# Key chunks that coincide with the query tiles, in an attention and feed-forward kernel on one core

## The chip, the cores and the metric

The kernel runs on one core of a Trainium2 chip. The core has a matrix engine (TensorE, "PE" in the profile, its loads of weights "PEld"), three engines for elementwise work (VectorE "DVE", ScalarE "ACT", GpSimd "POOL") and a queue that issues DMAs (SyncE, "SP"). TensorE writes only into eight PSUM banks of 128 partitions by 512 floats. The metric is the device time of one execution in microseconds; the program's own span, from its first to its last instruction, is what the trace covers.

## The reference

```python
scores = q @ k.T / sqrt(64)                    # 8 batches, 8 heads, 576 positions, 64 wide
decay  = cum[..., :, None] - cum[..., None, :] # cum = cumsum(log(clip(f)))
scores = where(causal, -1e9, scores + decay)
attn   = exp(scores - max); attn = attn / (sum(attn) + 1e-9)
x      = (attn @ v)                            # heads side by side: 4608 tokens, 512 wide
h      = x @ w_in                              # 512 to 2048
out    = softplus(h) @ w_out                   # 2048 to 512
```

All of it is float32. A product in which float32 precision is wanted is split: each operand is a rounded high part plus a low part, and three of the four part products are summed (a "fp32r" operand is a rounded part).

## The kernel before

The kernel is a list of operations, each with an engine (or a choice of engines), an estimated cost, its predecessors, and the buffers that it takes and gives back. A planner (`Plan.run`) walks this list with its estimated clocks and emits the operations in the order in which they would start; what it fixes is the order on each engine, and semaphores do the rest on the chip. So an operation's estimated cost (`on_turn`, `on_act`, `on_dve`, `on_pe`) changes the order, not the time that the chip takes.

The batches' heads come as jobs. Batch 0 is done in halves (`first`, `rest`, plain float32); batches 1 to 7 give 56 jobs `whole`, one head each. Between the steps of the jobs, units of the feed-forward part (`ffn_block`: ten blocks of 256 or 512 tokens, products of 512 columns into the banks `h` and `acc`) are let in by a budget. Their products stand between those of the heads in TensorE's queue.

A whole head runs thus. Five query tiles (`QT`, L249) of 64, 128, 128, 128, 128 rows are scored against all keys up to their own end (L756, L757, bank `s`), VectorE adds the mask and takes the row's extreme (L761), ScalarE takes the exponential into `p` (L781), and ScalarE, VectorE or GpSimd divides by the sum (L803, L805). Tile i ends at key 64, 192, 320, 448 or 576.

Then `weights(bi)` turns `p` round, one bank `b` at a time: `turn` (L849) transposes blocks on TensorE, with a block of `p` as the stationary operand and an identity (`ident`) as the moving one. `halves` is an identity whose halves are exchanged: a block turned against it lands 64 columns away, which is needed where a key chunk begins in the middle of a query tile. From the bank, `hi_part` (L861, copies at L211) makes the rounded high part `ph`, and `lo_part` the rest `pl` (L871) on VectorE. `output(gi)` (L891) multiplies the values `vhl` (high and low side by side, 128 columns, as the stationary operand) with `ph` and `pl` as the moving operands into a bank `o` (L911). Group 0 are queries 0 to 63, group 1 the rest. Two copies then put the result together in `x` (L934, L940).

Key chunks begin at 0, 128, 256, 384 and 512 and so lie across the query tiles. `banks` in `whole` (L541) lists, per bank, (first key, first query, last query, chunk of values):

- bank 0, the small one: keys 0 to 63 for queries 0 to 63, and keys 512 to 575 for queries 512 to 575, 64 columns each. Only 64 partitions are used, and the low part goes to partitions 64 to 127 of the same `ph64` tile (L868), so that one product takes both parts; for this the values' chunk `NCH` holds keys 0 to 63 twice (L615 to L618), and so does the last chunk of the padded `vR`.
- bank 1: keys 0 to 127, queries 64 to 575, 512 columns.
- bank 2: keys 128 to 255, queries 128 to 575, 448 columns.
- bank 3: keys 256 to 383 and 384 to 511, 320 and 192 columns.

Banks of PSUM named `att` (four) serve scores, transposes and outputs; `ph` and `pl` have three buffers each, `ph64` two. The values are loaded by three SyncE DMAs (L614, and two at L618) and split into high and low part (L687, L690). In the order of the list a head's first three banks are followed by group 0, the last bank and group 1, between the scores of the next head.

Of the kernel before, what the change touches and what calls it, by code (L numbers as in the profile page):

```python
# [10 lines left out]
F32 = mybir.dt.float32  # L11
U32 = mybir.dt.uint32
F32R = mybir.dt.float32r
# [34 lines left out]
class Plan:  # L48
# [161 lines left out]
def copy(e, out, in_):  # L210
    (e.tensor_copy if hasattr(e, "tensor_copy") else e.copy)(out, in_)  # L211
# [3 lines left out]
def tile_decay_attention_softplus_ffn(  # L215
# [18 lines left out]
    B, D, H, _, S = qkT.shape  # L234
    NT, DM = out.shape
    DFF = w_in.shape[1]
    P = 128
# [3 lines left out]
    NCH = vR.shape[3]  # L241
# [4 lines left out]
    LAG = 2  # L246
# [5 lines left out]
    BUFS = dict(T=2, att=4, h=2, acc=2, fe=4, ph=3, pl=3, ph64=2, gh=LAG + 1, gl=LAG + 1, xh=1, xl=1,  # L252
                x32=2, wl=2, vhl=3, vraw=1, raw=1)
    plan = Plan(BUFS | dict(T0=4, stat=4, p=2, xh0=1, xh1=1, xl0=1))
    add, give = plan.add, plan.give
# [7 lines left out]
    psum = ctx.enter_context(tc.tile_pool(name="psum", bufs=1, space=bass.MemoryType.PSUM))  # L263
# [15 lines left out]
    T = {}  # L279
# [15 lines left out]
    ps = [[cpool.tile([P, w], F32, name=f"p{i}_{w}") for w in PW] for i in range(2)]  # L295
# [242 lines left out]
    def whole(b, h):  # L538


        banks = [[(0, 0, 64, NCH), (512, 512, S, 4)], [(0, 64, S, 0)], [(128, 128, S, 1)],  # L541
                 [(256, 256, S, 2), (384, 384, S, 3)]]
        return dict(
            b=b, heads=[h], q=(0, S), k=(0, S), nv=NCH + 1,
            tiles=[(q0, n, 0, i, 0) for i, (q0, n) in enumerate(QT)],
            banks=banks, groups=[(0, 64, h, 0), (64, S, h, 64)],
        )
# [27 lines left out]
    def attention(job):  # L575
# [5 lines left out]
        plain = number < nplain  # L581
# [21 lines left out]

        def load_v():
            def v(e):
                shape = [P, (NCH + 1) * (2 if vtag == "vhl" else 1), D]
                vr = st["vr"] = buf(vtag, shape, f"vr{n}")[:, 0:nv]
                if pair:
                    e.dma_start(
                        out=vr[:, 0:4].rearrange("p (h c) d -> p h c d", h=2),  # L610
                        in_=vR[b, heads[0] : heads[0] + 2, :, 0:2].rearrange("h p c d -> p h c d"),
                    )
                else:
                    e.dma_start(out=vr[:, 0:NCH], in_=vR[b, heads[0]])  # L614
# [12 lines left out]

# [183 lines left out]


        parts = []
        used = {i: [] for i in range(len(banks))}
        tags = {}

        def weights(bi):
            spans, w = [], 0
            for key, lo, hi, vc in banks[bi]:
                spans.append((key, lo, hi, vc, w))  # L820
                w += hi - lo

# [26 lines left out]
            def turn(e):  # L849
                box["ps"] = bank("att", f"b{n}_{bi}")  # L850
                for x, at, one in blocks:
                    e.transpose(box["ps"][0 : x.shape[1], at : at + one.shape[1]], x, one)  # L852

            def keep(e):
                box["p"] = buf(tag, [P, 512], f"p{n}_{bi}", F32R)[:, 0:w].bitcast(F32)
                copy(e, box["p"], box["ps"][:, 0:w])

            more, size = ("64", P) if small else ("", 512)
            rows = 64 if small else P

            def hi_part(e):  # L861
                box["h"] = buf("ph" + more, [P, size], f"ph{n}_{bi}", F32R)[:, 0:w]
                copy(e, box["h"][0:rows], box["ps"][0:rows, 0:w])

            def lo_part(e):
                if small:
                    h = box["h"]
                    e.tensor_sub(h[64:P], box["ps"][0:64, 0:w], h[0:64].bitcast(F32))  # L868
                    return
                box["l"] = buf("pl", [P, size], f"pl{n}_{bi}", F32R)[:, 0:w]  # L870
                e.tensor_sub(box["l"], box["ps"][:, 0:w], box["h"].bitcast(F32))  # L871
# [6 lines left out]
            on = [on_act(w, psum=True), on_dve(w)]  # L878
# [12 lines left out]
        def output(gi):  # L891
            g0, g1, h, tok = groups[gi]
# [60 lines left out]
            if gi == len(groups) - 1:  # L953
                if plain:
                    give("T0", st["scores"])
                    if number == nplain - 1:
                        give("x32", cum_used)
                    give(st["vtag"], st["ends"])
                    for bi, ops in used.items():
                        give(tags[bi], ops)  # L960
                else:
                    give("T", st["scores"])
                    give("vhl", st["ends"])
                    for bi, ops in used.items():
                        if banks[bi][0][:3] == (0, 0, 64):
                            give("ph64", ops)
                        else:
                            give("ph", ops)
                            give("pl", ops)

        def loads():
# [492 lines left out]
```

## Time and profile before

| | |
|---|---|
| three executions | 1197.27, 1197.46, 1198.01 us (median 1197.46) |
| span of the profiled execution | 1196.2 us, granted TensorE clock 1.00 |
| TensorE matmuls | 6122 |
| chain that ended last | TensorE 77%, VectorE 12%, ScalarE 4%, DMA 3% of the span |
| DMA | 172.01 MB, mean 144 GB/s |

The span is the program's own; the time of an execution contains a little ahead of it and behind it, 1.3 us by the median. A row of the timeline has the start, the duration, the engine, the line, the operation, output<-inputs, the form, and the number of like instructions in a row. The duration of a pipelined matmul reaches past the start of the next one, so that TensorE's time is read from the distance of starts. In a row of groups stand, after the bar, the busy time in all, the mean of one in nanoseconds, and after the next bar the idle time of that engine just ahead of them with what ended it. In a row of stretches stand the bounds, the length, the busy time of each engine shown (with its number of instructions), the granted clock, the share of the DMA engines and GB/s.

### The profile page before, as it was taken

Reading aid. Unit: us, or ns where it says so; the run is one execution under the profiler, and the core shown is the slowest. Engines: PE = TensorE matmul, PEld = TensorE weight load, DVE = VectorE, ACT = ScalarE, POOL = GpSimd, SP = SyncE. Lnnn points to the kernel's source line nnn. Section 1 sums busy time; section 2 is a strip of 40 time slices with the busy share of each in tenths; the row PEclk is TensorE's granted clock in tenths of the full one; section 3 lists DMA queues with packets and bytes.
Section 4 is the critical chain, followed back from the end, with each engine's and each line's share of the span. In section 5 each row is a group of like instructions: output and inputs, shape, how many; then the busy total and the mean of one; then the engine's idle time right before and its main releaser. Section 6 shows DMA issues by size and latency. Waiting matters only on the chain.

```text
span 1196.2 us, 19275 instructions
## 1 busy us (share of the span) xinstructions
PE 1177.1 (98%) x6122; PEld 969.0 (81%) x6122; DVE 851.4 (71%) x2085; ACT 852.5 (71%) x2033; POOL 140.3 (12%) x143
## 2 busy tenths in 40 slices
PE   8999999999999999999999999999999999999998
PEld 6666678878888888888888888888888888888887
DVE  7998999897787778777787778677867773223322
ACT  6676888888886778678777778688867773444543
POOL 3200011111111110102011101011111110000000
PEclk9999999999999999999999999999999999999999
DMA  7855655545555645655565546555465524211210
GB/s 215 255 171 162 183 152 155 131 135 155 143 160 166 177 131 147 182 162 155 143 187 158 147 130 187 149 162 147 146 181 151 156 81 136 89 36 53 88 53 35
DMA packets 107317, 172.01 MB, mean 144 GB/s; under 512 B 20256, under 2 KB 77616, under 8 KB 107216
## 3 DMA queue, kind: packets, MB, share of 16 engines
q1 hardware_dynamic: 107200, 170.78, 50.1%
q8 instruction: 48, 0.79, 0.3%
q14 instruction: 53, 0.43, 0.1%
q10 hardware_dynamic: 16, 0.01, 0.0%
HBM read 126.49 MB, written 35.95 MB: 136 GB/s over the span
## 4 chain that ended last, share of the span: by engine, by line
PE 77%; DVE 12%; ACT 4%; DMA 3%; issue 2%; POOL 1%; SPq 0%; DVEq 0%; POOLq 0%; ACTq 0%
PE h L1069 27%; PE acc L1154 27%; PE b L852 7%; PE o L911 5%; PE s L756 3%; PE s L757 3%; DVE s L761 2%; PE h L1050 2%; PE acc L1173 1%; POOL p L805 1%; ACT p L781 1%; DMA raw<-in_qkT 1%; PE s L754 1%; PE o L905 1%; DVE T L712 1%
## 5 line engine op out<-in xcount | busy, mean ns | idle before, releaser
L1069 PE MATMUL h<-xh,wih 128*128 128x512 f32 (+1 forms) x576 | 229.1, 401 | 0.0
L781 ACT ACTIVATE p<-s,negm 128x288 f32<-128x288 f32 (+7 forms) x384 | 182.6, 478 | 55.0 <-DVE negm L761 53.4
L1069 PE MATMUL h<-xl,wih 128*128 128x512 f32 (+1 forms) x576 | 216.8, 379 | 0.0
L805 POOL TENSOR_SCALAR p<-p,rsum 64x64 f32<-64x64 f32 (+4 forms) x106 | 119.1, 1133 | 742.9 <-DVE rsum L794 292.5
L1116 DVE SCALAR_TENSOR_TENSOR h<-h,e 128x512 f32<-128x512 f32 x136 | 95.1, 699 | 138.1 <-ACT e L1108 137.3
L761 DVE CUSTOM_DVE_ANT_0 s<-s,cmask 128x288 f32<-128x288 f32 (+5 forms) x320 | 137.2, 439 | 74.1 <-PE s L757 63.6
L1102 ACT ACTIVATE e<-h 128x512 f32<-128x512 f32 x144 | 85.4, 594 | 112.7 <-PE h L1069 106.8
L1154 PE MATMUL acc<-woh_dt_float32r,gh 128*128 128x512 f32 x376 | 153.1, 407 | 0.1
L1069 PE MATMUL h<-xh,wl 128*128 128x512 f32 (+1 forms) x576 | 148.6, 380 | 0.0
L1154 PE MATMUL acc<-woh_dt_float32r,gl 128*128 128x512 f32 x376 | 147.3, 392 | 0.0
L1154 PE MATMUL acc<-wol_dt_float32r,gh 128*128 128x512 f32 x376 | 147.0, 391 | 0.0
L871 DVE TENSOR_TENSOR pl<-b,ph 128x512 fp32r<-128x512 f32 x168 | 110.8, 664 | 29.5 <-ACT ph L211 27.5
L211 ACT CAST ph<-b 128x512 fp32r<-128x512 f32 (+2 forms) x180 | 88.6, 500 | 50.8 <-PE b L852 47.4
L1069 PEld LDWEIGHTS h<-xh,wl 128*128 128x128 f32 x576 | 104.9, 188 | 21.5
L1069 PEld LDWEIGHTS h<-xh,wih 128*128 128x128 f32 x576 | 108.8, 189 | 15.5 <-PE b L852 0.2
L1069 PEld LDWEIGHTS h<-xl,wih 128*128 128x128 f32 x576 | 108.9, 189 | 14.7 <-DVE xl L1021 0.4
L852 PE MATMUL b<-ident,p 128*128 128x128 f32 (+1 forms) x728 | 117.8, 270 | 2.6 <-DVE x L940 0.6
L1124 DVE TENSOR_TENSOR gl<-h,gh 128x512 fp32r<-128x512 f32 x136 | 93.5, 687 | 36.6 <-ACT gh L211 36.0
L211 ACT CAST gh<-h 128x512 fp32r<-128x512 f32 x117 | 68.6, 586 | 53.6 <-DVE h L1116 48.1
L803 ACT ACTIVATE p<-p,rsum 128x320 f32<-128x320 f32 (+7 forms) x190 | 97.4, 573 | 5.1 <-DVE rsum L794 4.6
L756 PE MATMUL s<-T 128*64 128x64 f32 x336 | 98.5, 304 | 1.5 <-ACT p L781 1.3
L852 PEld LDWEIGHTS b<-ident,p 128*128 128x128 f32 (+1 forms) x728 | 86.1, 138 | 16.4 <-ACT p L781 2.1
(154 smaller groups left out, 2293.6 us busy)
## 6 DMA issues: line engine op xcount, KB each, us to landing
wl<-wil_d SPq DMA_DIRECT2D x72, 512.0 KB
raw<-in_qkT SPq DMA_DIRECT2D x112, 288.0 KB
g_d<-gh SPq DMA_DIRECT2D x84, 128.0 KB
g_d<-gl SPq DMA_DIRECT2D x84, 128.0 KB
vr<-in_vR SPq DMA_DIRECT2D x64, 160.0 KB
out<-ob SPq DMA_DIRECT2D x36, 256.0 KB
T<-T SPq DMA_DIRECT2D x56, 144.0 KB
sto<-in_w_out SPq DMA_DIRECT2D x11, 512.0 KB
```

Source lines behind the costliest of these rows:

```text
L211: (e.tensor_copy if hasattr(e, "tensor_copy") else e.copy)(out, in_)
L756: e.matmul(o, qA[:, q0:end], kA[:, a:z], start=True, stop=False)
L761: e.tensor_tensor_reduce(out=box["o"], in0=box["o"], in1=cmask[0:n_q, right - w : right], scale=-0.125, scalar=m0 if i else 3.0e38, op0=AL ...
L781: e.activation(o, box["o"], AF.Exp, bias=m1, scale=-1.0, accum_out=acc)
L803: e.activation(a, a, AF.Copy, scale=f_)
L805: e.tensor_scalar(a, a, f_, None, ALU.mult)
L852: e.transpose(box["ps"][0 : x.shape[1], at : at + one.shape[1]], x, one)
L871: e.tensor_sub(box["l"], box["ps"][:, 0:w], box["h"].bitcast(F32))
L1069: e.matmul(o, l, r, start=m == 0, stop=m == 11)
L1116: e.scalar_tensor_tensor(h, h, 0.0, box["e"], ALU.max, ALU.add)
L1124: e.tensor_sub(box["l"], box["t"], box["h"].bitcast(F32))
L1154: e.matmul(st["acc", tt], l, r[fc], start=first and m == 0, stop=last and m == 2,)
```

## The change

Key chunks of whole heads become 0 to 63, 64 to 191, 192 to 319, 320 to 447 and 448 to 575: the query tiles themselves. No block begins inside a query tile, and `halves` is left to the plain jobs. The first chunk has 64 keys and 512 later queries: its bank is `stacked` (high part in partitions 0 to 63, low part in 64 to 127, values doubled). Keys 0 to 63 for queries 0 to 63, the other part of that chunk, ride behind keys 320 to 447 in bank 1, with copies of their own (`first_hi`, `first_lo`). The values' chunk 0 holds keys 0 to 63 twice, the other chunks are put together from two neighbours of `vR`; there are five chunks in place of six. `ph` has four buffers, `ph64` is gone.

```diff
-    BUFS = dict(T=2, att=4, h=2, acc=2, fe=4, ph=3, pl=3, ph64=2, ...
+    BUFS = dict(T=2, att=4, h=2, acc=2, fe=4, ph=4, pl=3, ...
...
-        banks = [[(0, 0, 64, NCH), (512, 512, S, 4)], [(0, 64, S, 0)], [(128, 128, S, 1)],
-                 [(256, 256, S, 2), (384, 384, S, 3)]]
+        banks = [[(0, 64, S, 0)], [(320, 320, S, 3), (0, 0, 64, 0)], [(64, 64, S, 1)],
+                 [(192, 192, S, 2), (448, 448, S, 4)]]
         return dict(
-            b=b, heads=[h], q=(0, S), k=(0, S), nv=NCH + 1,
+            b=b, heads=[h], q=(0, S), k=(0, S), nv=NCH,
...
-                if nv > NCH:
-                    for r in (0, 64):
-                        e.dma_start(out=vr[r : r + 64, NCH], in_=vR[b, heads[0], 0:64, 0])
+                else:
+                    e.dma_start(out=vr[64:P], in_=vR[b, heads[0], 0:64])
+                    e.dma_start(out=vr[0:64, 1:NCH], in_=vR[b, heads[0], 64:P, 0 : NCH - 1])
+                    e.dma_start(out=vr[0:64, 0], in_=vR[b, heads[0], 0:64, 0])
...
-            more = (160, 1) if plain else (192, 3)
+            more = (160, 1) if plain else (160, 3)
...
+        def stacked(bi):
+            return not plain and banks[bi][0][:2] == (0, 64)
...
-            small = spans[0][:3] == (0, 0, 64)
+            small = stacked(bi)
...
-                for key, lo, hi, _, at in spans if small else reversed(spans):
+                for key, lo, hi, _, at in reversed(spans):
...
-                        second = q0 < lo and ti < nt - 1
+                        second = plain and q0 < lo and ti < nt - 1
...
-                            x = pt[pi][:, c : c + 64]
-                            one = halves
-                            if key == 0:
-                                x, one = x[0:68], ident[0:68, 0:68]
-                            blocks.append((x, key // 8, one))
+                            blocks.append((pt[pi][:, c : c + 64], at, ident))
+                        elif not plain and n_q < P:
+                            blocks.append((pt[pi][0:68, c : c + 64], at, ident[0:68, 0:68]))
...
-            more, size = ("64", P) if small else ("", 512)
-            rows = 64 if small else P
+            both = not plain and not small and spans[-1][0] == 0
+            rows, full = 64 if small else P, w - 64 * both
...
+            def stack_lo(e, a, z):
+                h = box["h"][:, a:z]
+                e.tensor_sub(h[64:P], box["ps"][0:64, a:z], h[0:64].bitcast(F32))
...
+            def first_hi(e):
+                copy(e, box["h"][0:64, full:w], box["ps"][0:64, full:w])
+
+            def first_lo(e):
+                stack_lo(e, full, w)
...
-            m = add(on_turn(len(blocks) - 0.48 * small), turn, after=need, takes=("att",))
+            m = add(on_turn(len(blocks) * (0.54 if small else 1)), turn, after=need, takes=("att",))
...
-                hp = add(on, hi_part, after=[m], takes=("ph" + more,))
-                ready = [hp, add(on_dve(w), lo_part, after=[hp], takes=() if small else ("pl",))]
+                hp = add(on, hi_part, after=[m], takes=("ph",))
+                ready = [hp, add(on_dve(full), lo_part, after=[hp], takes=() if small else ("pl",))]
+                if both:
+                    f_ = add([on_act(64, psum=True), on_dve(64)], first_hi, after=[hp])
+                    ready += [f_, add(on_dve(64), first_lo, after=[f_])]
                 give("att", ready[1:])
             for key, lo, hi, vc, at in spans:
-                parts.append((lo, hi, bi, vc, at, box, ready, small))
+                parts.append((lo, hi, bi, vc, at, box, ready, not plain and key == 0))
```

More of the change, by code (lines that the diff above doesn't have):

```diff
@@ L250, in tile_decay_attention_softplus_ffn @@
     QF, QR = [(0, 128), (128, 128)], [(256, 64), (320, 128), (448, 128)]
-    BUFS = dict(T=2, att=4, h=2, acc=2, fe=4, ph=3, pl=3, ph64=2, gh=LAG + 1, gl=LAG + 1, xh=1, xl=1,
+    BUFS = dict(T=2, att=4, h=2, acc=2, fe=4, ph=4, pl=3, gh=LAG + 1, gl=LAG + 1, xh=1, xl=1,
                 x32=2, wl=2, vhl=3, vraw=1, raw=1)
@@ L605, in v @@
             def v(e):
-                shape = [P, (NCH + 1) * (2 if vtag == "vhl" else 1), D]
+                shape = [P, NCH * (2 if vtag == "vhl" else 1), D]
                 vr = st["vr"] = buf(vtag, shape, f"vr{n}")[:, 0:nv]
@@ L612, in v @@
                     )
-                else:
-                    e.dma_start(out=vr[:, 0:NCH], in_=vR[b, heads[0]])
-                if nv > NCH:
-                    for r in (0, 64):
-                        e.dma_start(out=vr[r : r + 64, NCH], in_=vR[b, heads[0], 0:64, 0])
+                elif plain:
+                    e.dma_start(out=vr[:, 0:NCH], in_=vR[b, heads[0]])
+                else:
+                    e.dma_start(out=vr[64:P], in_=vR[b, heads[0], 0:64])
+                    e.dma_start(out=vr[0:64, 1:NCH], in_=vR[b, heads[0], 64:P, 0 : NCH - 1])
+                    e.dma_start(out=vr[0:64, 0], in_=vR[b, heads[0], 0:64, 0])
             vtag = "vraw"
@@ L856, in keep @@
                 copy(e, box["p"], box["ps"][:, 0:w])
[L858 to L859 removed]
+            both = not plain and not small and spans[-1][0] == 0
+            rows, full = 64 if small else P, w - 64 * both
             def hi_part(e):
[L862 to L863 removed]
+                box["h"] = buf("ph", [P, 512], f"ph{n}_{bi}", F32R)[:, 0:w]
+                copy(e, box["h"][0:rows, 0:full], box["ps"][0:rows, 0:full])
+            def stack_lo(e, a, z):
+                h = box["h"][:, a:z]
+                e.tensor_sub(h[64:P], box["ps"][0:64, a:z], h[0:64].bitcast(F32))
             def lo_part(e):
                 if small:
[L867 to L868 removed]
+                    stack_lo(e, 0, w)
                     return
[L870 to L871 removed]
+                box["l"] = buf("pl", [P, 512], f"pl{n}_{bi}", F32R)[:, 0:full]
+                e.tensor_sub(box["l"], box["ps"][:, 0:full], box["h"][:, 0:full].bitcast(F32))
+            def first_hi(e):
+                copy(e, box["h"][0:64, full:w], box["ps"][0:64, full:w])
+            def first_lo(e):
+                stack_lo(e, full, w)
             need = list(dict.fromkeys(need)) + halves_set
[L874 removed]
+            m = add(on_turn(len(blocks) * (0.54 if small else 1)), turn, after=need, takes=("att",))
             st.setdefault("turned", []).append(m)
@@ L877, in weights @@
                 give("p", st["turned"])
-            on = [on_act(w, psum=True), on_dve(w)]
+            on = [on_act(full, psum=True), on_dve(full)]
             if plain:
@@ L964, in output @@
                     for bi, ops in used.items():
[L965 to L968, printed above, removed]
+                        give("ph", ops)
+                        if not stacked(bi):
                             give("pl", ops)
```

## The prediction

> **What bounds the kernel now.** I read the page's line of engine totals first, then the table by stretches, of all instructions and (the last two rows) of VectorE's subtraction for the small bank at L868, of which each head has one, then TensorE's timeline in one steady stretch, where starts can be subtracted.
>
> ```profile
> PE 1177.1 (98%) x6122; PEld 969.0 (81%) x6122; DVE 851.4 (71%) x2085; ACT 852.5 (71%) x2033; POOL 140.3 (12%) x143
> ```
>
> ```profile
> 150.00:300.00 150.00, 145.12 (x871) 122.81 (x870) 133.28 (x341) 126.19 (x322) 20.08 (x16) 1.00 0.53 144
> 300.00:1005.00 705.00, 700.96 (x3731) 591.81 (x3731) 532.33 (x1311) 537.43 (x1315) 97.15 (x88) 1.00 0.55 155
> ```
>
> ```profile
> 140.00:300.00 160.00, 3.40 (x12) 1.00 0.54 145
> 300.00:1000.00 700.00, 12.47 (x44) 1.00 0.55 155
> ```
>
> The columns of a stretch are PE, PEld, DVE, ACT and POOL busy, then the granted clock (1.00 in all of them) and the DMA share. Twelve whole heads run before 300 us and 44 between 300 and 1000, one in 700/44 = 16 us. From 300 to 1005 us TensorE is busy 701.0 of 705 us, VectorE 76%, ScalarE 76%. From 150 to 300 the two are at 89% and 84%, and TensorE leaves 4.9 us. So **TensorE's instruction stream sets the end**, and the change is worth what it takes from that stream, less any hole that the two evacuating engines open in it. "Busy" overlaps pipelined matmuls, so I price TensorE by differences of starts.
>
> **The change, part by part.** The sum has four terms: transposes, value products, ScalarE/VectorE work, waits.
>
> *Transposes.* A head has 15 before and 15 after. What changes is their shape: before, 13 full blocks, one of 128 rows by 64 columns against `halves`, one of 68 by 64; after, ten full, four of 128 by 64 (bank 0), one of 68 by 64. Does a 64-column block cost half? These rows decide:
>
> ```profile
> 403.31 0.19 PE L911 MATMUL o<-ph,vhl 128*128 128x64 f32 x1
> 403.34 0.48 PE L1069 MATMUL h<-xh,wih 128*128 128x512 f32 x1
> 403.65 0.39 PE L1069 MATMUL h<-xl,wih 128*128 128x512 f32 x1
> ...
> 404.58 0.39 PE L1069 MATMUL h<-xl,wih 128*128 128x512 f32 x1
> 404.81 0.38 PE L852 MATMUL b<-halves,p 128*128 128x128 f32 x2
> 405.02 0.49 PE L852 MATMUL b<-ident,p 128*128 128x128 f32 x3
> 405.27 0.48 PE L1069 MATMUL h<-xh,wih 128*128 128x512 f32 x1
> 405.58 0.39 PE L1069 MATMUL h<-xl,wih 128*128 128x512 f32 x1
> ...
> 472.39 0.19 PE L911 MATMUL o<-ph,vhl 128*128 128x64 f32 x1
> 472.42 0.41 PE L852 MATMUL b<-halves,p 128*128 128x128 f32 x2
> 472.67 0.49 PE L852 MATMUL b<-ident,p 128*128 128x128 f32 x3
> 472.91 0.48 PE L1154 MATMUL acc<-woh_dt_float32r,gh 128*128 128x512 f32 x1
> 473.23 0.39 PE L1154 MATMUL acc<-wol_dt_float32r,gh 128*128 128x512 f32 x1
> ```
>
> The form reads stationary rows*columns, then the moving operand. A 512-column product takes 0.23 us (404.58 to 404.81). From 404.58 to 405.58 are 1.00 us: two such products and five transposes, so 0.54 for five, 0.108 each. From 472.39 to 473.23 are 0.84 us: a 64-column product, the same five transposes and one long product, which leaves 0.84 - 0.54 - 0.23 = 0.07 for the short one. From 403.31 to 403.65 are 0.34: the short product and a long one, which leaves 0.11. The short product streams in 0.03 (403.31 to 403.34); the rest is the wait for the next weights. So ordinary weights of 128 columns take 0.11, but the weights of a full transposing block are in place after 0.07. Transposes follow each other at 0.108, slower than that. What they wait for is then not the load of their stationary block but the streaming of the other operand, the identity, 128 columns wide. After the change that identity still has 128 columns: `one` is the whole `ident`, only the stationary block shrinks.
>
> ```profile
> 414.99 0.22 PE L852 MATMUL b<-ident,p 68*64 68x68 f32 x1
> 415.04 0.28 PE L852 MATMUL b<-halves,p 128*64 128x128 f32 x1
> 415.07 0.48 PE L1069 MATMUL h<-xh,wih 128*128 128x512 f32 x1
> 415.39 0.40 PE L1069 MATMUL h<-xl,wih 128*128 128x512 f32 x1
> ```
>
> The pair of bank 0 takes 415.39 - 414.99 - 0.23 = 0.17: about 0.06 for 68 moving columns and 0.11 for 128. It fits streaming, and does not exclude the other reading (0.06 for the second block's 64-column weights, 0.11 for the 128-column weights behind). By streaming a head costs fourteen times 0.108 plus 0.06, 1.57 us, before and after: **change 0**. By weights, each block would cost the load of the one behind it, 0.108 for a full one and 0.057 for one of 64 columns. In bank 0 one block before has such a follower, and three after; in bank 1 the small block goes first, its load beside the work ahead. That is 2 times 0.051, 0.10 per head, 5.7 us over 56 heads. I take 0, since 0.07 is measured on a transposing block itself, and keep -5.7 as the other end.
>
> [...]
>
> *Value products.* Before, ten per head; after, ten.
>
> ```profile
> 408.67 0.39 PE L911 MATMUL o<-ph,vhl 128*128 128x512 f32 x1
> ...
> 409.43 0.36 PE L911 MATMUL o<-pl,vhl 128*128 128x448 f32 x1
> 409.63 0.31 PE L911 MATMUL o<-ph,vhl 128*128 128x320 f32 x1
> ...
> 409.93 0.25 PE L911 MATMUL o<-ph,vhl 128*128 128x192 f32 x1
> ...
> 410.38 0.39 PE L1069 MATMUL h<-xl,wih 128*128 128x512 f32 x1
> ```
>
> Group 1 before takes 410.38 - 408.67 - 0.23 = 1.48 us. Its parts: 512 columns 0.23, 448 0.20 (409.43 to 409.63), 320 0.15 (two of them to 409.93), and 64 or 192 columns 0.11, where the next weights bind ((410.38 - 0.23 - 409.93)/2). After: bank 0 stacks its high and low part in one product of 512 (0.23); then 512 twice (0.46), 256 twice (between 0.11 and 0.15: 0.12 each, 0.24), 384 twice (between 0.15 and 0.20: 0.175 each, 0.35), 128 twice (0.11 each, 0.22). Sum 1.50. The change halves the first chunk's products but also gives up the stacked 64-column one and widens the others: 1472 columns twice and 128 once become 1280 twice and 576 once, 3072 and 3136 in all. **+0.02 per head, +1.1 us**; the interpolation bounds it between -0.05 per head (256 at 0.11, 384 at 0.15) and +0.13 (0.15 and 0.20), -2.8 to +7.3 us. Group 0 stays one 64-column product.
>
> *Evacuation.* Per head the copies go from 128 + 512 + 448 + 512 columns to 512 + 256 + 64 + 512 + 512, and from four of each kind to five.
>
> ```profile
> L211 ACT CAST ph<-b 128x512 fp32r<-128x512 f32 x102 | 59.8, 586 | 31.4 <-PE b L852 30.4
> L211 ACT CAST ph<-b 128x448 fp32r<-128x448 f32 x38 | 20.3, 533 | 18.8 <-PE b L852 16.7 <-PE o L911 2.1
> L211 ACT CAST ph<-b 64x128 fp32r<-64x128 f32 x40 | 10.0, 251 | 0.6 <-PE b L852 0.3
> L211 ACT COPY x<-o 64x64 f32<-64x64 f32 x56 | 11.6, 206 | 3.1 <-PE o L911 1.9
> L871 DVE TENSOR_TENSOR pl<-b,ph 128x512 fp32r<-128x512 f32 x112 | 77.0, 687 | 26.4 <-ACT ph L211 25.1
> L871 DVE TENSOR_TENSOR pl<-b,ph 128x448 fp32r<-128x448 f32 x56 | 34.7, 619 | 3.1 <-ACT ph L211 2.3
> L868 DVE TENSOR_TENSOR ph<-b,ph 64x128 fp32r<-64x128 f32 x56 | 15.9, 284 | 3.4 <-ACT ph L211 1.6
> L940 DVE TENSOR_TENSOR x<-o,x 64x64 f32<-64x64 f32 x56 | 12.2, 218 | 15.6 <-ACT x L211 14.9
> ```
>
> High copies on ScalarE: before 251 + 586 + 533 + 586 = 1956 ns; after 586 three times, 206 for 64 columns and 365 for 256 (on the line from 128 to 512): 2329, +373. Low parts on VectorE: before 284 + 687 + 619 + 687 = 2277; after 687 three times, 218, and 418 for 256 (between 284 and 687): 2697, +420. The split of values loses 64 of 384 columns, what 448 and 512 differ by: 53 on ScalarE and 68 on VectorE. Together +0.32 and +0.35 us per head, 18 and 20 us in all, or 1.5% of the span on each engine. Of a head's 16 us in the steady stretch each engine has a quarter free, near 4 us: the value and feed-forward products hide it. The cover is thin from 150 to 300 us.
>
> *Waits and queues.* Bank 1 is now evacuated in four steps (high 256, low 256, then high and low of 64 for the first tile), one behind the other where before the small bank had two; group 0's product waits for the last. Its scores bank is held some 0.6 us longer, and on the in-order engines the next copies queue behind it. Bank 0 now needs the scaled rows of tiles 1 to 4, before those of 0 and 4 alone; a late GpSimd scaling delays all four of its blocks. It also takes one of four `ph` buffers in place of one of two small ones, freed by the head's last value product; at 410.2 that is nearly 5 us ahead of the next head's bank 0 (414.99), so nothing. The planner counts bank 0 at 0.24 us where I expect 0.43; that shifts its order by fractions of a microsecond. SyncE issues three value loads per head as before, of 160 KB in all for 192, and nothing is moved past them. I put +0.5 us on all of this, between -3 (a luckier order; TensorE leaves 4 us in the steady stretch) and +8 (the rival below).
>
> **Sum.** 0 + 1.1 + 0.5 = +1.6. The profiled span is 1196.2 us, 1.3 below the median of the three times, 1197.46, the start and end around it; the change touches neither. 1197.5 + 1.6 is about **1199 us**.
>
> **Rivals.** *A, half-price blocks.* If the 64-column blocks do run at 0.057, TensorE loses 5.7 us, and with the other two terms the time is 1193.4. For it: the pair's 0.17 allows it. Against it: the 0.07. *B, the evacuating engines become the bound.* Twelve heads run by 300 us, where VectorE is at 89%; if it sets the pace there, 12 times 0.35 = 4.2 us come through. At the six later borders of a batch, where splits pile up on the same engines, a head's extra 0.67 on both could do so too, 4.0 us. With the products 1197.5 + 1.1 + 8.2 = 1206.8; half of it 1202.7. It decides once a copy comes later than TensorE's filler lasts. For it: VectorE's 133 of 150 us. Against it: a quarter free later. *C, nothing but another order*: the planner closes 3 of the 9 us that TensorE idles from 150 to 1005 us, 1195. For it: every bank changes its columns or its place in the list, so that the whole order is made anew. Against it: the holes lie where the other engines have more to do than before.
>
> **How the numbers follow.** Forecast (1196 to 1201) 0.50, A 0.13, B 0.27 (1201 to 1207), C 0.10 (1193 to 1196). The range goes from 1192 to 1206, and leaves out the outer parts of A and B, some 0.12. About 0.2%, 2.4 us, is what a measurement can tell from no change: faster means below 1195.1, slower above 1199.9. Faster: A and six tenths of C, 0.19. Slower: B and a fifth of the forecast, its upper end, 0.37. Same: 0.44. The likeliest case's own range is 1196 to 1201.
>
> **What would show it.** Starts of the four bank-0 transposes: 0.108 apart bears me out, 0.057 apart is A. Group 1's nine products should take 1.50 us. VectorE and ScalarE should be busy 18 to 20 us more each. For B, TensorE's idle between 150 and 300 us would grow past 4.9 us and the waits of L911 and of the transposes on VectorE would lengthen. I am wrong if the 0.07 came from weights fetched ahead of time, or if the new order closes or opens holes by more than 3 us.

## The result, and the profile after

| | before | after |
|---|---|---|
| executions | 1197.27 to 1199.2 us (4) | 1205.38 to 1209.99 us (4) |
| median | 1197.74 us | 1207.63 us |
| ratio, 95% interval | | 1.0080 [1.0068, 1.0092] |
| span of the profiled execution | 1196.2 us | 1206.3 us |

The change costs 9.9 us, 0.8%. One execution of e1 below (1648.14 us) and one of the kernel before beside it (1286.44 us) were slow, at mean granted clocks of 0.65 and 0.85, and are left out of the medians. The work of TensorE is the same, 6122 matmuls. The page's line of engine totals, and the same stretches as before (PE, PEld, DVE, ACT, POOL, clock, DMA share, GB/s):

```profile
PE 1182.3 (98%) x6122; PEld 969.1 (80%) x6122; DVE 878.1 (73%) x2150; ACT 866.8 (72%) x2107; POOL 111.9 (9%) x116
```

```profile
150.00:300.00 150.00, 142.32 (x843) 119.53 (x842) 136.14 (x347) 124.56 (x327) 18.39 (x16) 0.99 0.50 135
300.00:1005.00 705.00, 699.35 (x3703) 586.69 (x3702) 552.61 (x1362) 550.38 (x1378) 70.71 (x62) 1.00 0.54 151
```

VectorE has 26.7 us more work, ScalarE 14.3 us more, GpSimd 28.4 us less. From 150 to 300 us TensorE idles 7.7 us in place of 4.9 and starts 28 matmuls fewer. From 300 to 1005 it idles 5.7 in place of 4.0. Over the whole span its idle time grows by 4.9 us and its busy time, with as many matmuls, by 5.2. The value products (all instructions of one line: count, shortest, median and longest in ns, first and last start) tell where the time is lost, first before, then after:

```profile
L911 PE MATMUL o<-ph,vhl x336: 191/302/595, 151.5 to 1004.4; 128*128 128x64 f32 x112, 128*128 128x320 f32 x56
```

```profile
L926 PE MATMUL o<-ph,vhl x336: 192/332/628, 151.9 to 1014.5; 128*128 128x64 f32 x56, 128*128 128x512 f32 x56, 128*128 128x384 f32 x56
```

The first is 0.4 us later, the last 10.1, so nearly all of it arises among the whole heads. The first score products of three heads on TensorE's timeline, before and after:

```profile
286.41 0.19 PE L756 MATMUL s<-T 128*64 128x64 f32 x1
...
960.53 0.19 PE L756 MATMUL s<-T 128*64 128x64 f32 x1
977.71 0.19 PE L756 MATMUL s<-T 128*64 128x64 f32 x1
```

```profile
291.46 0.19 PE L757 MATMUL s<-T 128*64 128x64 f32 x1
...
969.84 0.19 PE L757 MATMUL s<-T 128*64 128x64 f32 x1
987.06 0.19 PE L757 MATMUL s<-T 128*64 128x64 f32 x1
```

At 286 us, twelve whole heads in, the lag is already 5.05 us; at 977 us it is 9.35. Between two borders of batches a head takes as long as before (17.18 us from 960.53 to 977.71, and 17.22 from 969.84 to 987.06): the other 4.3 us come in steps at the borders. The largest early step, on the timeline of all engines after (in brackets the idle time ahead of an instruction and who ended it):

```profile
250.36 0.60 PE L855 MATMUL b<-ident,p 128*128 128x128 f32 x4
250.49 0.95 DVE L1034 TENSOR_TENSOR xl<-x,xh 128x768 fp32r<-128x768 f32 x1
...
251.47 0.68 DVE L870 TENSOR_TENSOR ph<-b,ph 64x512 fp32r<-64x512 f32 x1
252.19 0.42 DVE L877 TENSOR_TENSOR pl<-b,ph 128x256 fp32r<-128x256 f32 x1
...
252.21 0.40 PE L757 MATMUL s<-T 128*128 128x288 f32 x1 [1.25 <-DVE ph L870]
...
252.63 0.22 DVE L870 TENSOR_TENSOR ph<-b,ph 64x64 fp32r<-64x64 f32 x1
...
253.40 0.69 DVE L877 TENSOR_TENSOR pl<-b,ph 128x512 fp32r<-128x512 f32 x1
...
254.14 1.12 PE L855 MATMUL b<-ident,p 128*128 128x128 f32 x4 [0.89 <-DVE pl L877]
```

The score product at 252.21 needs no data from `ph`. It needs a bank, and all four `att` banks are taken: by the transposes of banks 0, 1 and 2 (those of bank 2 are the four at 250.36) and by another tile's scores. The stacked low part of bank 0 (L870, 512 columns) gives one back, but on VectorE it stands behind a split for the feed-forward part (L1034). The transposes at 254.14 wait in the same way for bank 2's low part (L877). The first of these stretches before, and both after, all engines:

```profile
250.00:254.00 4.00, 4.00 (x22) 3.19 (x21) 3.82 (x8) 2.25 (x6) 0.00 (x0) 1.00 0.27 62
```

```profile
250.00:254.00 4.00, 1.77 (x10) 1.11 (x9) 3.90 (x8) 2.01 (x6) 0.00 (x0) 1.00 0.45 103
254.00:258.00 4.00, 3.86 (x14) 3.45 (x15) 3.74 (x10) 2.90 (x8) 0.00 (x0) 0.58 0.11 25
```

TensorE stands 2.2 us, and in the next 4 us its granted clock is 0.58, by 4 x 0.42 an estimated 1.7 us more. These 3.9 us are most of the early lag. Some of TensorE's longest waits over the whole execution (engine and line, whom it waited for: us, times, longest), before and after:

```profile
PE o L911 <- DVE x L940: 1.8, 4, 0.6
PE s L756 <- ACT p L781: 1.3, 3, 0.8
PE o L911 <- DVE ph L868: 1.2, 2, 0.6
```

```profile
PE o L926 <- DVE ph L870: 3.0, 7, 0.9
PE o L926 <- DVE x L955: 2.6, 6, 1.4
...
PE s L757 <- ACT p L782: 2.3, 5, 0.9
PE s L757 <- DVE ph L870: 1.2, 1, 1.2
...
PE s L757 <- DVE pl L877: 1.1, 3, 0.4
```

Three of the five rows after are copies out of a bank of transposes: the value products of the first row wait for the data, the score products of the fourth (it is the hole at 252.21) and fifth for the bank. L955 copies an output out of its bank, and L782 is the exponential, which reads the scores' banks. No wait of a matmul after the change is put down to a DMA.

These waits don't show the later loss whole. Between the rows of 286.41 and 977.71 before, and the same heads' 291.46 and 987.06 after, TensorE does as many matmuls (length, busy time, clock, DMA share, GB/s):

```profile
286.41:977.71 691.30, 687.83 (x3662) 1.00 0.56 156
```

```profile
291.46:987.06 695.60, 691.32 (x3662) 1.00 0.54 153
```

Of the 4.3 us between them only 0.8 are idle time. The other 3.5 are in its busy time, at full clock, and what they are the profile does not show.

**The copies.** Groups by line on VectorE and ScalarE, before and after (busy, mean ns, idle before):

```profile
L803 ACT ACTIVATE p<-p,rsum 128x320 f32<-128x320 f32 (+7 forms) x190 | 97.4, 573 | 5.1 <-DVE rsum L794 4.6
L211 ACT CAST ph<-b 128x512 fp32r<-128x512 f32 (+2 forms) x180 | 88.6, 500 | 50.8 <-PE b L852 47.4 <-PE o L911 2.1
L211 DVE CAST ph<-b 128x448 fp32r<-128x448 f32 (+2 forms) x44 | 22.4, 511 | 4.4 <-PE b L852 4.1
```

```profile
L804 ACT ACTIVATE p<-p,rsum 128x576 f32<-128x576 f32 (+7 forms) x222 | 111.0, 559 | 23.2 <-DVE rsum L795 22.9
L877 DVE TENSOR_TENSOR pl<-b,ph 128x256 fp32r<-128x256 f32 x168 | 100.6, 599 | 20.1 <-ACT ph L211 18.2
L211 ACT CAST ph<-b 128x512 fp32r<-128x512 f32 (+3 forms) x228 | 99.9, 454 | 38.3 <-PE b L855 26.7 <-DVE pl L877 5.1 <-DVE ph L211 4.2
L870 DVE TENSOR_TENSOR ph<-b,ph 64x512 fp32r<-64x512 f32 x112 | 50.4, 451 | 14.7 <-ACT ph L211 12.6
L211 DVE CAST ph<-b 128x512 fp32r<-128x512 f32 (+3 forms) x52 | 30.4, 588 | 8.0 <-PE b L855 7.6
```

Copies out of the transposes' banks were 88.6 + 22.4 us of high parts, and 112 x 0.687 + 34.7 + 15.9 = 127.5 of low parts by the prediction's rows: 238.5 in all. After they are 99.9 + 30.4 + 100.6 + 50.4 = 281.3, so 43 us more. ScalarE also does 32 scalings more (x222 for x190), while GpSimd's instructions fall from 143 to 116.

### The profile page after: what moved, and what is told of

Read it like the earlier page. It is cut to its first block, busy times and chain, and to the rows that moved or that the text cites. A ratio compares the mean times of both kernels' runs of the same rounds, so it can differ in the third digit from the quotient of the medians.

```text
span 1206.3 us, 19340 instructions
## 1 busy us (share of the span) xinstructions
PE 1182.3 (98%) x6122; PEld 969.1 (80%) x6122; DVE 878.1 (73%) x2150; ACT 866.8 (72%) x2107; POOL 111.9 (9%) x116
## 4 chain that ended last, share of the span: by engine, by line
PE 73%; DVE 15%; ACT 5%; DMA 4%; issue 2%; SPq 1%; POOL 0%; DVEq 0%; ACTq 0%; POOLq 0%
PE h L1082 26%; PE acc L1167 26%; PE b L855 6%; PE o L926 5%; PE s L757 2%; PE s L758 2%; DVE s L762 2%; PE h L1063 2%; PE s L755 1%; DMA raw<-in_qkT 1%; DVE pl L877 1%; ACT p L782 1%; DVE h L1129 1%; ACT p L804 1%; DVE xl L1034 1%
## 5 line engine op out<-in xcount | busy, mean ns | idle before, releaser
L782 ACT ACTIVATE p<-s,negm 128x288 f32<-128x288 f32 (+7 forms) x384 | 183.1, 479 | 48.5 <-DVE negm L762 46.6
L806 POOL TENSOR_SCALAR p<-p,rsum 128x448 f32<-128x448 f32 (+4 forms) x79 | 90.2, 1148 | 781.0 <-DVE rsum L795 563.6
L855 PE MATMUL b<-ident,p 128*128 128x128 f32 x952 | 139.5, 271 | 2.7 <-DVE pl L877 0.9
L855 PEld LDWEIGHTS b<-ident,p 128*128 128x128 f32 x952 | 109.5, 132 | 27.0 <-ACT p L804 2.5
L804 ACT ACTIVATE p<-p,rsum 128x576 f32<-128x576 f32 (+7 forms) x222 | 111.0, 559 | 23.2 <-DVE rsum L795 22.9
L211 ACT CAST ph<-b 128x512 fp32r<-128x512 f32 (+3 forms) x228 | 99.9, 454 | 38.3 <-PE b L855 26.7
L877 DVE TENSOR_TENSOR pl<-b,ph 128x256 fp32r<-128x256 f32 x168 | 100.6, 599 | 20.1 <-ACT ph L211 18.2
L211 ACT CAST gh<-h 128x512 fp32r<-128x512 f32 x129 | 75.5, 585 | 53.3 <-DVE h L1129 47.0
```

The source lines that it names most:

```text
L782: e.activation(o, box["o"], AF.Exp, bias=m1, scale=-1.0, accum_out=acc)
L804: e.activation(a, a, AF.Copy, scale=f_)
L806: e.tensor_scalar(a, a, f_, None, ALU.mult)
L877: e.tensor_sub(box["l"], box["ps"][:, 0:full], box["h"][:, 0:full].bitcast(F32))
```

## The experiments

Every variant is planned anew, so that its whole order may move. Four variants of the new layout that touch only an order or a buffer (e1, e3, e6, e7) lie 8.2 to 12.4 us above the kernel before, around the change's 9.9: among variants of this layout, 2 to 2.5 us are not assigned to a cause. Times are medians; the kernel before ran on the same chip, its median stands beside them, and losses and gains in the text are distances from it.

| run | from | time | before | ratio [95%] |
|---|---|---|---|---|
| e1 transposes priced in full | after | 1205.36 | 1197.12 | 1.0068 [1.0046, 1.0089] |
| e3 banks 0 and 1 exchanged | after | 1209.51 | 1197.12 | 1.0104 [1.0088, 1.0120] |
| e4 old layout in batches 1, 2 | after | 1201.84 | 1197.12 | 1.0039 [1.0025, 1.0053] |
| e6 first tile in a bank of its own | after | 1208.03 | 1197.56 | 1.0090 [1.0075, 1.0105] |
| e7 five `ph` buffers | after | 1205.96 | 1197.56 | 1.0073 [1.0057, 1.0089] |
| e2 more copies, off the banks | before | 1196.84 | 1197.12 | 0.9996 [0.9987, 1.0006] |
| e14 the same, high part on ScalarE | before | 1197.98 | 1197.11 | 1.0009 [0.9999, 1.0018] |
| e5 more copies, bank held | before | 1209.10 | 1197.56 | 1.0093 [1.0078, 1.0108] |
| e9 longer way to the products only | before | 1200.26 | 1197.38 | 1.0023 [1.0013, 1.0032] |
| e10 bank held only | before | 1203.12 | 1197.38 | 1.0044 [1.0028, 1.0061] |
| e8 three `att` banks | before | 1219.44 | 1197.56 | 1.0185 [1.0168, 1.0203] |
| e16 bank 0 needs all five tiles | before | 1197.37 | 1197.09 | 1.0002 [0.9992, 1.0011] |
| e17 GpSimd fills 384 columns | before | 1198.32 | 1197.09 | 1.0010 [1.0001, 1.0019] |
| e13 short low part | after | 1203.28 | 1197.11 | 1.0058 [1.0042, 1.0075] |
| e15 short high and low part | after | 1204.32 | 1197.75 | 1.0062 [1.0045, 1.0078] |
| e18 e15 and full prices | after | 1200.69 | 1197.09 | 1.0030 [1.0019, 1.0042] |
| e11 bank-freeing copies first | before | 1229.51 | 1197.38 | 1.0267 [1.0252, 1.0283] |
| e12 bank-freeing copies first | after | 1245.40 | 1197.38 | 1.0401 [1.0385, 1.0416] |

### Is it the order, or the engines' load? (e1, e2, e3, e4)

e1, in the kernel after:

```diff
-            m = add(on_turn(len(blocks) * (0.54 if small else 1)), turn, ...
+            m = add(on_turn(len(blocks)), turn, ...
```

> The changed kernel, with the planner's price of the stacked bank's four transposes at 4 x 0.109 us, as the trace has them, in place of 0.54 of that. Theory 1 (added copies on VectorE and ScalarE): the copies stay, so 1205 to 1210 us. Theory 2 (the order suffers from the wrong price): it comes back to 1198 to 1202 us. Theory 3 (any new order costs some us by chance): it moves by up to 5 us either way.

e2, in the kernel before: 192 of a head's 384 value columns are split a second time, in SBUF.

```diff
+            def v_hi2(e):
+                copy(e, st["vhl"][:, 0:3, 0:D], st["vr"][:, 0:3])
+            def v_lo2(e):
+                hi, lo = st["vhl"][:, 0:3, 0:D], st["vhl"][:, 0:3, D : 2 * D]
+                e.tensor_sub(lo, st["vr"][:, 0:3], hi.bitcast(F32))
```

> The kernel before, in which the split of the values does 192 of its 384 columns a second time, high and low: about 0.3 us more on ScalarE or VectorE and 0.35 us more on VectorE per whole head, off the banks of PSUM and with the old layout. Theory 1: the added work alone costs what the change costs, 1203 to 1209 us, with the holes at 150 to 300 us and at the borders of the batches. Theory 2 (bank order, chain of four copies, price): 1197 to 1199.5 us, hidden. Theory 3: within 3 us of 1198, without a pattern.

e3, in the kernel after: the first two banks exchanged.

```diff
-        banks = [[(0, 64, S, 0)], [(320, 320, S, 3), (0, 0, 64, 0)], ...
+        banks = [[(320, 320, S, 3), (0, 0, 64, 0)], [(0, 64, S, 0)], ...
```

> The changed kernel, with the bank of keys 320 to 447 and of the first tile ahead of the stacked bank, so that the first bank of a head needs the scaled rows of tiles 0, 3 and 4 alone. Theory 1: 1205 to 1210 us. Theory 2 (the first bank waits for all four tiles, and GpSimd loses scalings to ScalarE for it): 1198 to 1203 us, and GpSimd back from 79 scalings to about 100. Theory 3: up to 5 us either way.

e4, in the kernel after: batches 1 and 2, 16 heads, in the old layout.

```diff
+        old = b <= 2
+        if old:
+            banks = [[(0, 0, 64, NCH), (512, 512, S, 4)], [(0, 64, S, 0)], [(128, 128, S, 1)],
+                     [(256, 256, S, 2), (384, 384, S, 3)]]
```

> Old layout for the 16 whole heads of batches 1 and 2 (to about 370 us), new layout from batch 3 on; one ph64 buffer in place of two. Theory 1 with its price mostly where VectorE is at 90%: the lag of 5 us of the first twelve heads is gone and that of the later borders stays, 1200 to 1204 us. If the price lies in every head alike, 40 of 56 heads pay: 1204 to 1206 us.

The full price gives back 1.7 us, no more than the scatter, and the other bank order nothing. e4 is 4.7 us above the kernel before and so gives back 5.2, which agrees with where the trace puts the early lag. The surprise is e2. Its added groups, and its stretches:

```profile
L695 DVE TENSOR_TENSOR vhl<-vr,vhl 128x192 fp32r<-128x192 f32 x56 | 21.2, 379 | 0.5
...
L211 DVE CAST vhl<-vr 128x192 fp32r<-128x192 f32 x35 | 12.0, 343 | 0.6 <-ACT vhl L211 0.5
```

```profile
150.00:300.00 150.00, 144.56 (x873) 123.50 (x872) 137.16 (x357) 126.20 (x328) 19.01 (x15) 1.00 0.52 142
300.00:1005.00 705.00, 701.19 (x3734) 592.06 (x3733) 552.48 (x1394) 542.97 (x1324) 84.13 (x81) 1.00 0.54 155
```

VectorE is as busy as after the change, even a little busier from 150 to 300 us (137.2 for 136.1), and TensorE loses nothing. The load of the engines, as first put, is not the cause.

### Load in the bank's way (e5, e9, e10, e8, e14)

e5, in the kernel before: 192 columns of bank 1's high and low part are made a second time out of the bank, ahead of its release and of the products.

```diff
+            def hi_again(e):
+                copy(e, box["h"][:, 0:192], box["ps"][:, 0:192])
+            def lo_again(e):
+                h = box["h"][:, 0:192].bitcast(F32)
+                e.tensor_sub(box["l"][:, 0:192], box["ps"][:, 0:192], h)
...
+                if bi == 1:
+                    ready.append(add(on_dve(192), lo_again, after=ready[1:]))
```

> The kernel before, in which 192 columns of bank 1's high and of its low part are copied a second time: the work of the second run again (about 0.31 us and 0.35 us per head), but between the transposes and the products, with the scores bank held for it. Theory P (a scores bank of PSUM is held longer, so that the next scores, transposes and outputs find none free): 1201 to 1206 us. Theory Q (the fourth ph buffer is scarcer than the separate small one was) and theory R (group 0 waits for bank 1's four copies): 1196 to 1199 us, as the same work cost nothing elsewhere.

e9 rewrites the same columns of `ph` and `pl` in place once the bank is released; the products wait. e10 reads the bank twice more into a spare tile; only the release waits. The cut is e10's.

```diff
-                give("att", ready[1:])
+                held = ready[1:]
+                if bi == 1:
+                    h2 = add([on_act(192, psum=True), on_dve(192)], hi_again, after=held)
+                    held = [add(on_dve(192), lo_again, after=[h2])]
+                give("att", held)
```

> The kernel before; bank 1 is given back as before, and then 192 columns of its ph and pl are rewritten in place (ph copied onto itself, zero subtracted from pl), so that the value products wait about 0.7 us longer, as in the fifth run, but no scores bank is held for it. If theory P means the bank's time: 1196 to 1200 us. If it is the longer way from the transposes to the value products: 1205 to 1209 us.

> The kernel before; after the low part, 192 columns of bank 1 are read twice more into a tile that nobody uses, and the bank is given back after that. The value products don't wait, the scores bank is held as long as in the fifth run. If the bank's time is the price: 1205 to 1209 us. If the longer way to the products is: 1196 to 1200 us. Both near 1203 us: the two share it.

e8, in the kernel before:

```diff
-    BUFS = dict(T=2, att=4, ...
+    BUFS = dict(T=2, att=3, ...
```

> The kernel before with three scores banks in place of four. Theory P: far slower, 1215 us or more, with the holes where the changed kernel has them. If the banks are not what is short: within 5 us of 1198.

e14 is e2 with the second high part on ScalarE alone (`add(on_act(3 * D), v_hi2, after=[vh])`).

> The second run again, with the repeated high part of the values (192 columns) forced onto ScalarE: about 0.3 us more of ScalarE and 0.35 us more of VectorE per head, off the banks. If added work off the banks is hidden whichever engine has it: 1196 to 1199 us. If it is ScalarE's work that costs: 1201 to 1206 us.

The added groups of e5, with the transposes that stood behind them:

```profile
L852 PE MATMUL b<-halves,p 128*128 128x128 f32 x176 | 39.7, 278 | 4.9 <-DVE pl L871 3.4 <-DVE pl L878 1.4
...
L878 DVE TENSOR_TENSOR pl<-b,ph 128x192 fp32r<-128x192 f32 x56 | 19.7, 351 | 0.6
...
L211 ACT CAST ph<-b 128x192 fp32r<-128x192 f32 x42 | 13.4, 320 | 1.2 <-DVE ph L211 0.3
```

About 40 us of copies cost nothing when they read SBUF (e2, e14: 21.2 + 12.0 above and 7.2 on ScalarE), and 38 us of like copies (these two rows and 5.0 of high parts on VectorE) cost 11.5 us when a bank and the products wait for them. e10 and e9 part this: 5.7 us for the bank held, 2.9 us for the longer way, and 3 us more when both come together, which puts e5 above the range expected for it. By an estimate from the granted clocks (the span times what they lack of 1.000) the clock can account for these 3 us: the executions of e5 ran at mean granted clocks of 0.995 to 0.997, some 4.8 us of 1206 by their mean, those of e10 at 0.997 to 1.000, some 1.2 us, and those of e9 at 0.999 to 1.000, 0.3 us. In e8, with one bank fewer, the time rises by 21.9 us. Its longest waits of TensorE are those of a score product for a bank that an output copy gives back:

```profile
PE s L756 <- DVE x L940: 7.3, 8, 2.8
```

e10 has the same kind of hole at the same place as the kernel after, with the same sequel (stretches of all engines):

```profile
250.00:254.00 4.00, 1.70 (x9) 1.42 (x10) 3.65 (x10) 2.66 (x7) 0.00 (x0) 0.91 0.60 152
254.00:258.00 4.00, 4.00 (x17) 3.49 (x16) 2.18 (x7) 1.06 (x2) 0.00 (x0) 0.66 0.02 6
```

e14 clears another suspect. Its long stretch:

```profile
300.00:1005.00 705.00, 702.19 (x3742) 593.39 (x3741) 556.40 (x1379) 549.99 (x1360) 61.37 (x66) 1.00 0.54 155
```

GpSimd is busy 61 us, less than the 71 after the change, and VectorE and ScalarE as much as there, yet TensorE is at its fullest. That ScalarE took over scalings from GpSimd is not the cause.

### Which hold is it in the new layout? (e13, e15, e18, e17)

e13, in the kernel after: bank 0's stacked low part for 128 of its 512 columns; GpSimd fills the rest of those partitions with zeros, so that the first chunk's low part is left out for most queries. e15 leaves out the high part there too. e18 is e15 with e1's prices. e17 puts the fill alone into the kernel before.

```diff
-                    stack_lo(e, 0, w)
+                    stack_lo(e, 0, 128)
...
+            def zero_rest(e):
+                e.memset(box["h"].bitcast(F32)[64:P, 128:w], 0.0)
...
-                ready = [hp, add(on_dve(full), lo_part, ...
+                lo_cost = on_dve(128 if small else full)
+                ready = [hp, add(lo_cost, lo_part, ...
```

> The changed kernel; the stacked bank's low part is subtracted for 128 of its 512 columns only and the other 384 are zero, set by GpSimd (so the first chunk's low part is left out for most queries). The bank is held about 0.4 us less per head, and VectorE's work on banks is back near that of the kernel before. If the work on the held banks is the price in the new layout too: 1198 to 1203 us. If not: 1205 to 1209 us.

> The last but one run, with the stacked bank's high part cut to 128 of 512 columns as well (high and low part of the first chunk are left out for most queries; GpSimd writes zeros there). The work with scores banks held is then below that of the kernel before on both engines. If held work explains the price whole: 1195 to 1199 us. If a part of it lies in the layout itself (five copies in place of four, what each bank waits for): 1200 to 1203 us.

> The run before last but one (first chunk's high and low part cut to 128 columns) with the planner's price of the stacked bank's transposes at 4 x 0.109 us. If the rest is an order made with a wrong price: 1197 to 1200 us. If it lies in the layout: 1202 to 1205 us.

> The kernel before, with a memset of 128 x 384 by GpSimd per head into a tile that nobody uses, as e15 has one. If e15's 6 us come from this helper and not from the layout: 1200 us or more. If not: 1196 to 1199 us.

e13 is 6.2 us above the kernel before and gives back 3.7 of 9.9; its interval and the change's overlap. e15, at 6.6, gives back no more, a miss. In e18 the true price, worth 1.7 us or nothing by itself, gives 3.0 us on top: 3.6 us are left, between the two ranges expected, and the fill is about 1 of them by e17 (where nothing waits for it). Each step alone, of 3 to 4 us, is little above the scatter; the 6.3 us of both together, two thirds of the loss, and the 4.6 us between e1 and e18, which differ only in bank 0's shorter copies, their prices and the fill, are clear of it.

### Other suspects (e6, e7, e16)

e6 gives the first tile's 64 x 64 block, and with it group 0, a bank and a small buffer of its own. e7 sets `ph=5` in place of 4. e16, in the kernel before, lets the first bank wait for all five scaled tiles (`need = list(st["norm"])`).

> The changed kernel, with keys 0 to 63 for queries 0 to 63 in a bank and a small ph64 tile of their own (as before) in place of behind keys 320 to 447: same columns copied, but group 0 waits for two short copies, and a head takes five scores banks in place of four. Theory R: 1198 to 1202 us. Theory P: no better, 1205 to 1210 us, since a fifth bank is taken. Theory Q: a ph buffer is held no longer, 1204 to 1208 us.

> The changed kernel with five ph buffers in place of four. Theory Q: 1198 to 1202 us. Theories P and R: 1205 to 1209 us.

> The kernel before; in the planner the first (small) bank of a head waits for the scaled rows of all five tiles in place of tiles 0 and 4, as the changed kernel's first bank waits for four. If what e15 left (6 us) comes from that: 1200 to 1204 us, and GpSimd loses scalings. If not: 1196 to 1199 us.

None of the three moves the time by more than the scatter. Group 0's later copies, the shared `ph` buffers and the four scaled rows that bank 0 needs are no main cause.

### A planner in a hurry (e11, e12)

Both let the planner take a copy that gives an `att` bank back, and the one just before it, 0.25 us ahead of its turn.

```diff
-                if s and (best is None or (s[0], op.rank) < best[0]):
-                    best = (s[0], op.rank), op, s
+                if s and (best is None or (s[0] - op.hurry, op.rank) < best[0]):
+                    best = (s[0] - op.hurry, op.rank), op, s
```

> The kernel before, in which the planner puts copies that give a scores bank back, and those just ahead of them, forward by 0.25 us against other work of their engine. If banks are what is short: less waiting in the stretch from 150 to 300 us, 1192 to 1197 us. Otherwise within 3 us of 1198, either way.

> The changed kernel with the same preference of 0.25 us for what gives a scores bank back. If banks are what is short: 1199 to 1204 us. Otherwise 1205 to 1210 us.

Both miss by far. The longest wait of TensorE in e11:

```profile
PE acc L1159 <- DVE gl L1129: 5.9, 6, 1.6
```

The feed-forward products, which cover the heads' waits, now wait themselves for their low part `gl`. That is 6 us of 32. By the same estimate another 17 are a lower clock: e11's profiled execution ran at a mean granted clock of 0.986 over 1227.8 us. Where the rest arises was not followed further.

## Why the prediction was wrong

*Transposes: right.* In a steady stretch of TensorE's timeline after:

```profile
403.88 0.88 PE L855 MATMUL b<-ident,p 128*64 128x128 f32 x7
404.52 0.48 PE L1082 MATMUL h<-xh,wih 128*128 128x512 f32 x1
404.83 0.40 PE L1082 MATMUL h<-xl,wih 128*128 128x512 f32 x1
```

From 403.88 to 404.83 are 0.95 us: less 0.23 for one long product, 0.72 for seven transposes, which is six at 0.109 and the small one at 0.06. At half price the four 64-column blocks would leave about 0.5. The starts of the four, the prediction's own sign, lie 0.11 us apart in all 56 heads of the trace (0.108 to 0.113), and those of full blocks before 0.109 by the median. Against the identity's 128 columns a block of 64 columns takes what a full one takes, and rival A is out.

*Value products: right.* Group 1 on the same timeline:

```profile
414.84 0.61 PE L926 MATMUL o<-ph,vhl 128*128 128x512 f32 x2
...
416.27 0.45 PE L1082 MATMUL h<-xh,wih 128*128 128x512 f32 x1
416.56 0.39 PE L1082 MATMUL h<-xl,wih 128*128 128x512 f32 x1
```

416.56 - 414.84 - 0.23 = 1.49 us, forecast 1.50, before 1.48. So +0.6 us in place of +1.1.

*Evacuation: prices right, share half right.* The prediction's 0.373 and 0.420 us per head are 44.4 us over 56 heads; the trace has 43. VectorE took more of it, since the planner gave it 52 high parts in place of 44. In all, VectorE is 26.7 and ScalarE 14.3 us busier, for a forecast of 20 and 18.

***"The value and feed-forward products hide it"*: the step that failed**, and with it the +0.5 us for all waits (between -3 and +8): of the 9.9 us, less 0.6 for the products, 9.3 came through. The step counted how much of each engine was free, and by that count the work is hidden: e2 and e14 show it on either engine. But these copies run while one of four scarce banks is held, and the next scores or transposes on TensorE need one. The prediction named one bank, bank 1 ("held some 0.6 us longer"), and gave it no price of its own. The hold was too small as well: from the first transpose of a bank to the end of its last copy, summed over a head's four banks in the trace, it grows from 10.5 to 12.0 us in the first twelve heads and from 8.75 to 10.35 in the others. The copies alone make 0.79 of these 1.5 us (44.4/56). Bank 0 makes about half of it (0.7 us in the first twelve heads, 0.8 in the others): high and low part of 128 columns took 251 + 284 ns, those of 512 take 571 + 684. The price of a hold is what e5 and e10 measured on the old layout, 6 to 11 us for 38 us of copies, with the lower clock behind the holes in it, and the change adds 43. In the new layout, e18 against e1 gives 4.6 us for the copies of bank 0 alone.

*Rival B: right in place and nearly in size, wrong in reason.* It put 4.2 us between 150 and 300 us and 4.0 at later borders; measured are 4.6 by 291 us (5.05 less the 0.4 with which the value products begin) and 4.3 more by 987 us. But it charged the engines' whole work where they are busiest, and e2 loads VectorE just as much there without loss. The early part comes out through the banks, and about 1.7 us of it is the lower clock behind the hole; of the later 4.3 us, 3.5 do not show as waits.

*The planner's price for bank 0* (0.24 us for 0.43) was called "fractions of a microsecond". Alone it is within the scatter (e1, 1.7 us), but with the hold shortened it is worth 3.0 us (e18 against e15), a little more than the scatter.

*Open:* some 2.4 us of the new layout remain in e18 with the fill's 1.2 taken off, and no run settles them; the value products can be 0.6 of them. Of TensorE's 5.2 us of added busy time, the clock's 1.7 and the products' 0.6 are accounted for, the rest not.

## What to carry to other kernels

Price a copy out of PSUM by whether somebody waits for its bank, not by how idle its engine is: 40 us of copies off the banks were free; 38 us on one of four banks cost 5.7 when only the bank's release waited for them, and 11.5 when the products did too. Columns taken from a matmul need not save time: a 64-column stationary block against a 128-column identity took what a full one did, 0.11 us. Where a planner's prices set the order, a wrong price can hide behind another limit, so measure its worth again once that limit is gone.

## What the runs showed of the chip

A hole of 2.2 us spread over 4 us of TensorE's work was followed by a granted clock of 0.58 over 4 us after the change, and of 0.66 in e10 behind a like one (busy 1.70 of 4). Cut to the drop itself, after the change:

```profile
253.97:257.38 3.41, 3.24 (x12) 2.95 (x13) 3.19 (x9) 2.31 (x6) 0.00 (x0) 0.50 0.01 3
```

The clock stood at one half for 3.41 us, by which an estimated 1.7 us are lost: value products of 512 columns start 0.43 us apart there (at 255.54, 255.97 and 256.39 us), and 0.23 at a clock of 1.00 (415.29 to 415.52). The longest single idle stretch in the 4 us ahead of it was 1.25 us, with four transposes and a few products around it. e10's profiled execution has two drops: its granted clock is 0.91 from 250 to 254 us and 0.66 from 254 to 258, and again 0.62 from 266 to 270. In e2 the stretch from 250 to 254 us held 3.18 us of work, and the clock stayed at 1.00, there and in the next 4 us. How much work 4 us hold does not tell by itself whether a drop follows: e13's 2.89 us (from 250 to 254 us) were followed by a clock of 1.00 over the next 4 us, e10's 2.97 (from 262 to 266) by 0.62. What brings a drop, these runs do not settle.

The clock also goes with part of the scatter of the changed kernel: its four executions took 1205.38, 1207.19, 1208.07 and 1209.99 us at mean granted clocks of 1.000, 0.998, 0.999 and 0.995.
